# Weight-decoding arithmetic opened to GpSimd, with another hand-written order, in an attention and gated-MLP kernel

## The chip, the cores and the metric

The kernel runs on one core of one Trainium2 chip. The metric is device time in microseconds (us); lower is better. TensorE is called PE, VectorE DVE, ScalarE ACT, GpSimd POOL and the engine that issues most transfers SP. The kernel before was timed three times.

## The reference, cut to what matters

Attention over 8 batches, 8 heads, 576 positions and 64 channels per head, with a decay that is summed along the sequence, and then a gated MLP on the 512 joined channels:

```python
cum = np.cumsum(np.log(np.clip(f, 1e-4, 1.0)), axis=-1)
scores = q @ k.T / 8 + cum[:, None] - cum[None, :]      # causal, then a softmax
x = attn @ v                                            # (8, 576, 512) over all heads
gate = sigmoid(sum_k conv_w[k] * shifted(x, k))         # 5 taps along the sequence
out = (gate * (x @ w_val)) @ w_out
```

`w_val`, `w_out` (both 512 x 512) and `conv_w` (5 x 512) arrive as 64-bit floats, which no engine computes with. The kernel reads each as two 32-bit words and makes of them a high and a low 32-bit part, so that products can be taken in three passes of the fast `fp32r` format.

## The kernel before, in words

The 64 (batch, head) rows are 32 pairs of heads, i = 0 to 31; four pairs make one batch. For a pair, PE makes scores in PSUM banks (class S), DVE adds the decay and finds each row's minimum ("red", line 457), ACT takes exponentials (SX, line 461), PE transposes them (PT, lines 502 and 526), ACT or DVE copies the transposes out of PSUM (class PE, line 259), PE multiplies by v (PV), and DVE scales the result into `x` (line 576). From pair 4 on the loaded q and k (`Xr`) are first split into `Xh` (TH, a cast, line 259) and `Xl` (TL, a subtraction, line 373). `x` is split likewise into `xh` and `xl` (line 583). The convolution (cv, lines 264, 266 and 615) and a tanh give the gate. After four pairs the MLP of a batch follows: first product (Mv), gating (line 647), a split into `hh` and `hl` (line 661), second product (Mo), a copy out (O) and a store. "sel" (lines 466, 468 and 301) writes the causal mask into a loaded decay tile.

`decode` and `plan_w` unpack the weights, in eight chunks of 128 x 512 (four of `w_val`, class wv, then four of `w_out`, class wo). For one chunk: "low" (line 704, ACT) converts the low words, "m" (706, DVE) masks bits, "mid" (708, DVE) adds the two, "y" (710, DVE) masks the high words, "expo" (712, ACT) scales them, "h" (714, DVE) and line 716 (DVE) build the high part and its power of two, then "hi" (a cast, line 259, ACT or DVE) and "lo" (line 741, POOL or DVE) write the parts into `wall`. `conv_w` goes through the same `decode` with 20 columns (class cw). All chunks share the scratch tiles `wz` and `wh`, so they follow one another.

Nothing decides at run time: `plan.add` collects 2932 nodes with the engines that may run each (`dve`, `act` and `pool` allow one, `any_` several, with a duration in us), and `Plan.order` replays TABLE, a string that names for each of its 2572 entries the node, its engine and its PSUM bank. Each engine therefore works through a fixed queue, and waits at its head for whatever a node depends on. The durations in the code are not read when the table is replayed.

Of the kernel before, what the change touches and what calls it, by code (L numbers as in the profile page):

```python
# [9 lines left out]
I32 = mybir.dt.int32  # L10
AF = mybir.ActivationFunctionType
# [34 lines left out]
0010s30240z40930740K40r30V40d30C20B10D20E20t30520630430F10G20e20b30m000H20f10I20a30J20q010h20u30c328002340i20j40N20M12R40P22900O20Q10g10R22a02d22j0565  # L46
740T10S25942b22e10U32f22c12s012q22h20x32g11442o22t02k20X13-42m22p10Y22642i10-22x0700Z20_10p032u22n12l11022r12v11122A0342z21332D065121340122C22E12B12F2
1f42y12w21721612G043722V037602H13b23523c12I41921822K41a12X04642Q11b22W03811c21d12M43021e33613i022O43223112-24241h13k042Y24043311q43921k23a11i21l13x001
1j22Z13d051m22_13j23e03z15543l21n23o114443A0473f24844c33C11p33B13p22T43y13m14b037403q21B43g13n33r21s13u0561o13s25j33w14d24x013v14f24e13h24m0654g14h34a
34i20y34B0377044k24j14C24n34l14o23D034D14q23O003E14p14s23H43N14t21v23F44u14y24r15d45i043761t24z17244v21u23L41w17f24H0123J44w15k24I15b40l054J14A25l14E0  # L50
215m27441x24K044G14U14F25o33Q017g37d15r25n14L25p24O45t0425s11y20v34M43P25u35q15I0355h37645v21z13R25E065x25K13U205z34S45J17e30n053S15F27840o034Q43V25G1
8b47i35A23W27h053673T35B15f45w15C28h43t13X25y14V041A37l25D17j27m15H21D13Y27n35O0237c35Q10w37k15P25R004W25L0325S17q25_15T44X051E25N15V47o25M11F21M47r17
s0341G27p14Y27t37H0275X48q34_107w27u25Z47D057J15028j47I17y36k078d47v18r37z27E27A19m462025127F18f47B27x152260037C14Z17G25321H14-37K0456327N0066127L17Q0
17R16426c037P17U47O27-16526f068o17S48n27a41I266106d09q48p31K16g06727Y47M16e26n025419o46h29z16827W48s063546i19u41J28t23Z19s46j38u26o06928v16l01L38w29B1
7_066p28x18y36m29A38B281078z28C16a26q18E38028A19C38D0408228S05285168H2ax48F26s038U19E31X48628J38T18O019y38318726r38G16t08P21O16v058K28438Q1882az46w08L
16u26b18M21R29D01234aB48N16x2aK38I18l4892aM1aD48Y0059H28Z19Z068-19F29I19O0058R29G19-29J3aL3cB49M28V0219_19K28X18W28_069P39N16D01902aP39Q26y19349S26A02
9R19929149U39T1aF49X26B01P29Y19V29L11Q2cD4a10549W1aN2a70679741S16E0a02954a811T2a919w4a31aO006376z2a21cQ11U26F2aJ3aa041V1cO3aQ29c01ak1aS2ab2aT1aU36C2ae
49a04cR3aV2ac49d2aW1aX2cF46G1a40169b2a-3aR11W3aZ0329g24a51dM4b12a61bc001a_2cJ4aY19h2b33ai4be16H3b806b429i2ag4b511Z1cH4al01b629j2cP3b71dQ4bd1b92aH4b019
k2ba1bf003cT31-2b21cS04567202bh1bb2dZ2bg11_2211bi032an00cW2d-3bk1cU2cX1am2bj1cL4d1025cY3cV1ao2222dS4bl00dO4bm2bv16N03cN2cZ2eX4ar10c_2bn42326I04d01as2d
23bp4c-1253d52241d32dc06at2d41d736O0d_1d82da2d61au2e03d916J0dd2db1av2de1f34br49e2dg0528a1e22e101067bt46K19f3di2e_46P1f14dj024df26Q4e32fa3by03dk1dU4dl1  # L60
e526L4dh1e73bw02e61ea2e82eb1bz2ec005e91ed2bx2ap1dp03g64ee2dm076eg2ef16S02eZ4dz2ei3dn1e41fb26T0do1el2dY3dq2bC16ej2dr4bA1bD2dt4en03eh1f81bE26X01em1eo2f9
3ek1dv46Y0bF2ep1dx46U1bG2fd3ga4aq3er034g84fc02567et2es16Z1gl3eu040fe2dA03fg2ff1eq2fh1fi3dC01bB3dB2ev1fj2ew1fl2ex032dD2eA04fo2ey1fn010dE2eK1eB2gj1f72eC
4fr2bL03ez2fk1eE4fp2bI05fs1dW4ft3fm1gm3bM0i54dG16f54bJ0bN29l1eG4fw2gk3dH2bQ04bK2fy02dI2bO1bT05fu2fx1fz2bP3fv1bR0fq1dJ2id4fA1bU0eI4dF3dK2i94fC010bV2i74
gn06723bS2fD1go3ge4fB2bW2gc4fF015gr26V4eL04gp26-4gs1fG2gt3fE1eN07gu2gq1eM2gw2ii2gy064gx1eO2gz3fL00aw1fH2ik3jg4fI073gv1gC2bY05gg4gA2fV1bX2bZ0bH1gE2fM1b
_02fJ2ij3eR10fP4gF2b-2ib4c707gB1gH2eS2gG1fN4c00gI1in3gD1gi3eT2c406il3fK1c12gJ03eU2c21c50fT4dL1gK2jt3fR4c80eV2gL1ji4c32gN052jk4im03401gO1gM2c92c62jv2gQ
# [754 lines left out]
```

## Time and profile before

| | us |
|---|---|
| median of three runs | 496.66 (496.4 to 498.02) |
| the profiled execution | 495.69 |
| span of its instructions | 494.0 |
| PE busy | 473.0 |
| DVE busy | 430.0 |
| ACT busy | 345.6 |
| POOL busy | 192.1 |

The profiled execution is 1.69 us longer than its span, and 0.97 us shorter than the median. A row of a view by lines gives line, engine, operation, output<-inputs, shapes, count, then busy us and mean ns of one, then the engine's idle time just before and what ended it. PE's busy time counts modelled ends of pipelined matmuls, so a PE that is shown busy can still be held up between them.

### The profile page before, as it was taken

Reading aid. Unit: us, or ns where it says so; the run is one execution under the profiler, and the core shown is the slowest. Engines: PE = TensorE matmul, PEld = TensorE weight load, DVE = VectorE, ACT = ScalarE, POOL = GpSimd, SP = SyncE. Lnnn points to the kernel's source line nnn. Section 1 sums busy time; section 2 is a strip of 40 time slices with the busy share of each in tenths; the row PEclk is TensorE's granted clock in tenths of the full one; section 3 lists DMA queues with packets and bytes.
Section 4 is the critical chain, followed back from the end, with each engine's and each line's share of the span. In section 5 each row is a group of like instructions: output and inputs, shape, how many; then the busy total and the mean of one; then the engine's idle time right before and its main releaser. Section 6 shows DMA issues by size and latency. Waiting matters only on the chain.

```text
span 494.0 us, 13906 instructions
## 1 busy us (share of the span) xinstructions
PE 473.0 (96%) x5136; PEld 411.3 (83%) x5136; DVE 430.0 (87%) x1181; ACT 345.6 (70%) x937; POOL 192.1 (39%) x249
## 2 busy tenths in 40 slices
PE   5898999899999999999999999999999999999996
PEld 3666788778899888998898888998889988998985
DVE  5999999999889889989899999979998989988661
ACT  4999989898867767578687667577887776662010
POOL 4242748564554642272334423144312644340100
PEclk9999999999999999999999999999999999999999
DMA  5785665576365456555663474744636474510112
GB/s 183 248 262 160 196 200 197 149 210 201 135 205 203 124 150 227 133 175 175 161 176 94 146 225 159 226 131 152 202 90 195 156 195 137 191 53 27 42 44 106
DMA packets 35012, 79.57 MB, mean 161 GB/s; under 512 B 5056, under 2 KB 5312, under 8 KB 34944
## 3 DMA queue, kind: packets, MB, share of 16 engines
q1 hardware_dynamic: 34864, 78.54, 52.3%
q8 instruction: 40, 0.66, 0.6%
q14 instruction: 28, 0.23, 0.2%
q10 hardware_dynamic: 80, 0.15, 0.1%
HBM read 68.93 MB, written 9.73 MB: 159 GB/s over the span
## 4 chain that ended last, share of the span: by engine, by line
PE 67%; DVE 12%; ACT 10%; DMA 6%; issue 3%; SPq 1%; POOL 1%; DVEq 0%; ACTq 0%; POOLq 0%
PE banks L244 59%; PE banks L502 6%; DVE banks L457 5%; ACT P L461 4%; ACT pt L259 2%; DMA x<-rzd 2%; PE banks L526 2%; DMA out_dram<-ot 1%; SPq L270 1%; DVE banks L615 1%; DVE negm L457 1%; DVE pt L259 1%; DMA rzd<-pl 1%; DMA Xr<-in_x_dram 1%; ACT Pl L461 1%
## 5 line engine op out<-in xcount | busy, mean ns | idle before, releaser
L461 ACT ACTIVATE P<-banks,negm 128x512 f32<-128x512 f32 (+3 forms) x256 | 134.0, 529 | 37.6 <-DVE negm L457 36.6
L457 DVE CUSTOM_DVE_ANT_0 banks<-banks,dm 128x512 f32<-128x512 f32 (+1 forms) x240 | 115.3, 504 | 11.6 <-POOL dm L466 3.6
L244 PE MATMUL banks<-xh,wall 128*128 128x288 f32 x512 | 110.7, 299 | 0.5 <-DVE pt L259 0.5
L259 ACT COPY pt<-banks 128x512 f32<-128x512 f32 (+1 forms) x163 | 81.2, 532 | 27.7 <-PE banks L502 19.5
L466 POOL TENSOR_SCALAR_AFFINE_SELECT dm<-dm 128x256 f32<-128x256 f32 x83 | 35.8, 433 | 160.4 <-DVE negm L457 121.6
L244 PE MATMUL banks<-pt,vt 128*64 128x128 f32 (+1 forms) x1280 | 93.5, 297 | 1.7 <-DVE h L647 1.3
L244 PE MATMUL banks<-wall,hh 128*128 128x512 f32 x288 | 91.0, 397 | 0.5 <-DVE x L576 0.4
L244 PEld LDWEIGHTS banks<-xh,wall 128*128 128x128 f32 x512 | 84.2, 188 | 3.0 <-DVE pt L259 0.8
L244 PEld LDWEIGHTS banks<-pt,vt 128*64 128x64 f32 x1280 | 75.5, 137 | 10.4 <-ACT P L461 1.9
L615 DVE SCALAR_TENSOR_TENSOR banks<-x,cw,banks 128x576 f32<-128x576 f32 x96 | 78.5, 817 | 2.5 <-ACT banks L264 1.7
L373 POOL TENSOR_TENSOR Xl<-Xr,Xh 128x640 fp32r<-128x640 f32 (+1 forms) x44 | 66.5, 1516 | 34.3 <-ACT Xh L259 19.4
L244 PE MATMUL banks<-xl,wall 128*128 128x288 f32 x256 | 75.5, 295 | 0.0
L502 PEld LDWEIGHTS banks<-ident,P 64*128 64x128 f32 x1280 | 49.5, 138 | 18.3 <-ACT P L461 6.2
L502 PE MATMUL banks<-ident,P 64*128 64x64 f32 x1280 | 58.1, 226 | 6.0 <-ACT P L461 2.9
L244 PEld LDWEIGHTS banks<-wall,hh 128*128 128x128 f32 x288 | 51.9, 188 | 11.2 <-DVE x L576 0.5
L244 PE MATMUL banks<-wall,hl 128*128 128x512 f32 x144 | 56.3, 391 | 0.0
L461 ACT ACTIVATION_READ_ACCUMULATOR P<-banks,negm 128x1 f32 x256 | 51.9, 203 | 0.0
L244 PE MATMUL banks<-Xh 64*128 64x512 f32 (+2 forms) x224 | 51.8, 375 | 0.1
L244 PEld LDWEIGHTS banks<-xl,wall 128*128 128x128 f32 x256 | 48.1, 188 | 0.3
L244 PE MATMUL banks<-Xh,Xl 64*128 64x512 f32 (+2 forms) x224 | 45.9, 327 | 0.5 <-POOL Xl L373 0.3
L583 POOL TENSOR_TENSOR xl<-x,xh 128x576 fp32r<-128x576 f32 x24 | 34.3, 1431 | 29.6 <-DVE xh L259 22.2
L244 PE MATMUL banks<-Xl,Xh 64*128 64x512 f32 (+2 forms) x224 | 45.6, 325 | 0.0
(97 smaller groups left out, 758.3 us busy)
## 6 DMA issues: line engine op xcount, KB each, us to landing
Xr<-in_x_dram SPq DMA_DIRECT2D x32, 608.0 KB
dm<-decd SPq DMA_DIRECT2D x60, 256.0 KB
vt<-in_v_dram SPq DMA_DIRECT2D x32, 320.0 KB
x<-rzd SPq DMA_DIRECT2D x64, 144.0 KB
out_dram<-ot SPq DMA_DIRECT2D x36, 256.0 KB
dl<-decd SPq DMA_DIRECT2D x60, 144.0 KB
ot<-in_w_val_dram SPq DMA_DIRECT2D x2, 512.0 KB
wu<-in_w_val_dram SPq DMA_DIRECT2D x2, 512.0 KB
```

The source lines that it names most:

```text
L244: nc.tensor.matmul(out, lhsT=lhsT, rhs=rhs, start=start, stop=stop)
L259: (eng.copy if eng is nc.scalar else eng.tensor_copy)(out=out, in_=in_)
L270: lambda e: (nc.sync if e == "SP" else nc.scalar).dma_start(out=out, in_=in_), reads, writes, **kw)
L373: eng.tensor_tensor(out=Xl[r][:, a:e], in0=Xr[r][:, a:e], in1=Xh[r][:, a:e].bitcast(F32), op=ALU.subtract)
L457: nc.vector.tensor_tensor_reduce(out=sl, in0=sl, in1=add, op0=ALU.add, op1=ALU.min, scale=-0.125, scalar=3.0e38, accum_out=negm[r][:, col])
L461: nc.scalar.activation(out=dst[:, o:o + ext], in_=bank(key)[:, c0:c0 + ext], func=AF.Exp, bias=negm[r][:, col], scale=-1.0, accum_out=zs[r ...
L466: eng.affine_select(out=t, in_=t, pattern=[[0, 2], [-1, P]], base=0, channel_multiplier=1, compare_op=ALU.is_ge, fill=-BIG)
L502: nc.tensor.transpose(out=bank(key[a])[:, c:c + D], in_=Pt[ms[h]][sl, BOFF[b] + P * j:BOFF[b] + P * j + P], identity=ident[sl, sl])
L526: nc.tensor.transpose(out=t[0:m, 512 * h + D * j:512 * h + D * j + D], in_=Pl[r][sl, P * j:P * j + m], identity=ident[sl, sl])
L583: any_("xl", {"POOL": 1.4, "DVE": 0.67}, p, lambda eng: eng.tensor_tensor(out=xl[s], in0=xv, in1=xh[s][:, :].bitcast(F32), op=ALU.subtract ...
L615: eng.scalar_tensor_tensor(out=gt if n == KC - 1 else sums, in0=src, scalar=wt_, in1=sums, op0=ALU.mult, op1=ALU.add)
```

## The change

Three of `decode`'s steps may run on POOL too, and the casts "hi" and the entries for TH and "lo" get other durations in the planner's terms. The load of `conv_w` gets another due time. The table is another one: of the 2572 entries 286 name another engine, and order and banks differ.

```diff
-            any_("TH", {"ACT": c / 1200.0 + 0.09, "DVE": c / 1920.0 + 0.08, "POOL": c / 640.0 + 0.42}, i + 0.02 * n, hi, [("Xr", r)], [("Xh", r, n)])
+            any_("TH", {"ACT": c / 1200.0 + 0.09, "DVE": c / 1920.0 + 0.08, "POOL": c / 1280.0 + 0.27}, i + 0.02 * n, hi, [("Xr", r)], [("Xh", r, n)])
...
-        act(cls, a, p, lambda: nc.scalar.activation(
-            out=zz, in_=y.bitcast(mybir.dt.uint32), func=AF.Copy, scale=2.0 ** -52), kl + kg, kz)
+        g = n / 1280.0 + 0.25
+
+        def low(eng):
+            if eng is nc.scalar:
+                eng.activation(out=zz, in_=y.bitcast(mybir.dt.uint32), func=AF.Copy, scale=2.0 ** -52)
+            else:
+                eng.tensor_scalar(out=zz, in0=y.bitcast(mybir.dt.uint32), scalar1=2.0 ** -52, scalar2=None, op0=ALU.mult)
+
+        def mid(eng):
+            if eng is nc.vector:
+                eng.scalar_tensor_tensor(out=zz, in0=m, scalar=2.0 ** -20, in1=zz, op0=ALU.mult, op1=ALU.add)
+            else:
+                eng.tensor_scalar(out=h, in0=m, scalar1=2.0 ** -20, scalar2=None, op0=ALU.mult)
+                eng.tensor_tensor(out=zz, in0=h, in1=zz, op=ALU.add)
...
+        any_(cls, {"ACT": a, "POOL": g}, p, low, kl + kg, kz)
...
-        dve(cls, two, p, lambda: nc.vector.scalar_tensor_tensor(
-            out=zz, in0=m, scalar=2.0 ** -20, in1=zz, op0=ALU.mult, op1=ALU.add), kh + kz + kg, kz)
+        any_(cls, {"DVE": two, "POOL": g + n / 440.0 + 0.1}, p, mid, kz + kg, kz + kh)
...
-        act(cls, a, p, lambda: nc.scalar.activation(
-            out=y, in_=y, func=AF.Relu, scale=8.0, bias=ebias[0:y.shape[0]]), [*kl, ("ebias",)], kl)
+        any_(cls, {"ACT": a, "POOL": 2 * g}, p, expo, [*kl, ("ebias",)], kl)
...
-        load("cw", 0.1, p, cwu, conv_w.bitcast(I32), (), [("cwu",), ("h32", 1), *kl])
+        load("cw", 0.31, p, cwu, conv_w.bitcast(I32), (), [("cwu",), ("h32", 1), *kl])
...
-            any_(nm, {"ACT": 0.52, "DVE": 0.34}, p, lambda eng, hi=hi: copy(eng, hi, wh), kh + kg, [(nm + "h", c)])
+            any_(nm, {"ACT": 0.55, "DVE": 0.34, "POOL": 0.67}, p, lambda eng, hi=hi: copy(eng, hi, wh), kh + kg, [(nm + "h", c)])
```

Read entry by entry, the two tables differ in engines as follows (out and back in, whole table; in brackets the part ahead of the first Mo, entry 637 of before and 636 of after):

| class | ACT to POOL | DVE to POOL | POOL to ACT | POOL to DVE | ACT to DVE | DVE to ACT |
|---|---|---|---|---|---|---|
| low, 128 x 512 | 5 (5) | | | | | |
| low, 20 columns | 1 (1) | | | | | |
| hi, 128 x 512 | 2 (2) | | | | | |
| mid, 128 x 512 | | 1 (1) | | | | |
| TH | 15 (3) | 6 (1) | 6 (1) | | 3 | 5 (1) |
| TL | | 12 (1) | | 10 (1) | | |
| hl and xl | | 13 | | 9 | | |
| sel | | 31 (4) | | 29 (5) | | |
| class PE, 512 columns | | | | | 23 (1) | 27 (3) |
| class PE, 256 columns | | | | | 9 | 13 (2) |
| class PE, 73 x 128 | | | | | 7 (1) | 11 (3) |
| cv | | | | | 5 | 6 (1) |
| O, hh, xh | | | | | 18 | 18 |

The step "expo" stays on ACT everywhere. One 64-column copy of the mask at the start goes from POOL to DVE. On SP the load of `conv_w` becomes the first one, ahead of the half of `f` that was first. On POOL the 20-column "low" stands ahead of the making of `ident`. In PE's queue the number of neighbours that use the array in different ways (the planner's `mode`) is 238 before and 233 after.

## Rows read from the trace of the kernel before

**Rows 1.** The page's head and its first part, whole span.

```profile
span 494.0 us, 13906 instructions
PE 473.0 (96%) x5136; PEld 411.3 (83%) x5136; DVE 430.0 (87%) x1181; ACT 345.6 (70%) x937; POOL 192.1 (39%) x249
```

**Rows 2.** Windows: stretch, its length, busy us (count) of PE, PEld, DVE, ACT, POOL.

```profile
10.00:110.00 100.00, 91.49 (x1072) 73.73 (x1071) 94.39 (x275) 91.18 (x244) 49.32 (x60) 1.00 0.67 201
110.00:440.00 330.00, 326.45 (x3674) 289.94 (x3673) 298.63 (x824) 242.35 (x668) 133.09 (x161) 1.00 0.55 166
440.00:494.00 54.00, 50.24 (x380) 44.58 (x378) 32.03 (x73) 8.95 (x22) 4.29 (x4) 1.00 0.14 51
```

**Rows 3.** The chain that ended last, by line: from 10 to 110, then 120 to 450.

```profile
by line: PE banks L244 25.8%; DVE banks L457 11.7%; ACT P L461 10.8%; DMA x<-rzd 7.9%; ACT pt L259 5.9%; issue 5.7%; PE banks L502 3.8%; ACT Pl L461 3.2%; DVE banks L615 2.7%; DVE negm L457 2.2%; DVE gate L615 1.9%; DMA rzd<-pl 1.6%; ACT ba
...
by line: PE banks L244 66.0%; PE banks L502 7.4%; DVE banks L457 3.4%; issue 3.1%; ACT P L461 2.7%; PE banks L526 1.9%; ACT pt L259 1.8%; DMA out_dram<-ot 1.8%; DMA Xr<-in_x_dram 1.1%; SPq L270 1.0%; DMA dm<-decd 1.0%; DMA dl<-decd 0.8%; DV
```

**Rows 4.** The start: pieces of that chain, SP's first issue, PE's second stretch.

```profile
1.44 3.07 DMA h<-in_conv_w_dram
4.54 0.89 DVE gate L706
9.17 0.52 DVE gate L335
...
0.81 0.58 SPq L270 DMA_DIRECT2D Pl<-in_f_dram  x1
...
10.33 2.29 PE L244 MATMUL banks<-gate,gate 64*128 64x512 f32 x12
```

**Rows 5.** ACT's groups by line and form, whole span.

```profile
L704 ACT ACTIVATE gate<-ot 128x512 f32<-128x512 uint32 x4 | 2.8, 690 | 0.8 <-DMA ot<-in_w_val_dram 0.8
L259 ACT CAST wall<-gate 128x512 fp32r<-128x512 f32 x8 | 5.0, 630 | 0.0
L259 ACT CAST Xh<-Xr 128x576 fp32r<-128x576 f32 x14 | 9.5, 676 | 0.0
L259 ACT COPY pt<-banks 128x512 f32<-128x512 f32 x118 | 66.9, 592 | 20.7 <-PE banks L502 12.7 <-DVE pl L259 3.2 <-PE banks L526 3.1
L259 ACT COPY pt<-banks 128x256 f32<-128x256 f32 x45 | 15.8, 374 | 7.0 <-PE banks L502 6.8
L264 ACT ACTIVATE banks<-x,cw 128x576 f32<-128x576 f32 x21 | 15.7, 749 | 1.2 <-DVE x L576 0.7 <-ACT P L461 0.2
```

**Rows 6.** DVE's groups by line and form, whole span.

```profile
L708 DVE SCALAR_TENSOR_TENSOR gate<-gate 128x512 f32<-128x512 int32 x8 | 5.5, 685 | 0.0
L259 DVE COPY pt<-banks 128x512 f32<-128x512 f32 x42 | 28.2, 683 | 2.9 <-PE banks L502 2.0 <-ACT pt L259 0.7
L259 DVE COPY pt<-banks 128x256 f32<-128x256 f32 x19 | 7.9, 416 | 0.0
L615 DVE SCALAR_TENSOR_TENSOR banks<-x,cw,banks 128x576 f32<-128x576 f32 x96 | 78.5, 817 | 2.5 <-ACT banks L264 1.7
L468 DVE TENSOR_TENSOR dm<-dm,tri 128x256 f32<-128x256 f32 x37 | 15.8, 427 | 0.5
```

**Rows 7.** POOL's groups by line and form, whole span.

```profile
L259 POOL CAST Xh<-Xr 128x576 fp32r<-128x576 f32 x9 | 6.1, 683 | 0.0
L741 POOL TENSOR_TENSOR wall<-gate,ot 128x512 fp32r<-128x512 f32 x4 | 5.2, 1297 | 10.7 <-DVE ot L716 10.7
```

**Rows 8.** Timeline near 5 us: a POOL fill, then a 20-column DVE step.

```profile
5.08 0.31 POOL L317 MEMSET gate<- 128x256 f32 x1
...
5.76 0.16 DVE L710 TENSOR_SCALAR h<-h 128x20 int32<-128x20 int32 x1
```

**Rows 9.** PE's timeline: the first product after transposes, and its successor.

```profile
87.82 0.40 PE L244 MATMUL banks<-xh,wall 128*128 128x288 f32 x1
88.06 0.30 PE L244 MATMUL banks<-xl,wall 128*128 128x288 f32 x1
```

**Rows 10.** PE's groups by line and form: the score products that read `Xl`.

```profile
L244 PE MATMUL banks<-Xh,Xl 64*128 64x512 f32 x56 | 11.5, 398 | 0.5 <-POOL Xl L373 0.3 <-DVE Xl L373 0.2
```

More of the change, by code (lines that the diff above doesn't have):

```diff
@@ L50 @@
[L50 to L53, printed above, removed]
@@ L98 @@
[L98 to L101 removed]
+0010b30z40240c30d30740r30K40V40630932R40C20B30430D20E20F10u30m000a30G20e20520f10q010H20x30I20g10J20h228002340t20i20M10N20j40P22902640O20Q12a00R22j0562
@@ L102 @@
+2DQ0Gy2HC01DM2Iq2Gz2HA02Gu2GA1HD2IA04DJ2Iu016IB1IK2Ir003IC4Iv1Fi2Ix045IE4Dq1Fj3Iz2DS01Fp1HB2Ea05DN1HE2It1II4DO2Iy1IG4DT0Iw1Is2HF3I-04HG22DR2E000DU2HH2
+IN07IL06IO2DV2HI2IX07IM2IP2DX01DW2IQ3J306E10I_0E21DY0E34J02HJ2E500DZ2HK2D-4Eb0IR12HL1IY0Je01IZ2IS2J607IT2Jb04J12J40J22J70Jc0J82J52E60J92IU2Jf0Ja2E71Ec
+1Jj07E84IV2Ed4Jm06Jd2IW1Jg2Jn0Jh2Ji2Jk0Jr01Jo2Jl2Jp2JG04Jq2Js0Jw06Jt2Ju4JB01Jx0JC0Jy2Jz4JL06JD1JE4JH0JM0JI2JJ4JN1JO4
 """
@@ L703, in decode, with expo @@
         a = n / 1200.0 + 0.145
-        act(cls, a, p, lambda: nc.scalar.activation(
-            out=zz, in_=y.bitcast(mybir.dt.uint32), func=AF.Copy, scale=2.0 ** -52), kl + kg, kz)
+        g = n / 1280.0 + 0.25
[10 more added lines that the diff above has]
+                eng.tensor_tensor(out=zz, in0=h, in1=zz, op=ALU.add)
+        def expo(eng):
+            if eng is nc.scalar:
+                eng.activation(out=y, in_=y, func=AF.Relu, scale=8.0, bias=ebias[0:y.shape[0]])
+            else:
+                eng.tensor_scalar(out=y, in0=y, scalar1=896.0 * 2.0 ** 20, scalar2=896.0 * 2.0 ** 20, op0=ALU.max, op1=ALU.subtract)
+                eng.tensor_scalar(out=y, in0=y, scalar1=8.0, scalar2=None, op0=ALU.mult)
+        any_(cls, {"ACT": a, "POOL": g}, p, low, kl + kg, kz)
         dve(cls, one, p, lambda: nc.vector.tensor_scalar(
             out=m, in0=hw, scalar1=0x1FF, scalar2=None, op0=ALU.bitwise_and), uk + kg, kh)
-        dve(cls, two, p, lambda: nc.vector.scalar_tensor_tensor(
-            out=zz, in0=m, scalar=2.0 ** -20, in1=zz, op0=ALU.mult, op1=ALU.add), kh + kz + kg, kz)
+        any_(cls, {"DVE": two, "POOL": g + n / 440.0 + 0.1}, p, mid, kz + kg, kz + kh)
         dve(cls, one, p, lambda: nc.vector.tensor_scalar(
             out=y, in0=hw, scalar1=0x7FFFFE00, scalar2=None, op0=ALU.bitwise_and), uk, kl)
-        act(cls, a, p, lambda: nc.scalar.activation(
-            out=y, in_=y, func=AF.Relu, scale=8.0, bias=ebias[0:y.shape[0]]), [*kl, ("ebias",)], kl)
+        any_(cls, {"ACT": a, "POOL": 2 * g}, p, expo, [*kl, ("ebias",)], kl)
         dve(cls, two, p, lambda: nc.vector.scalar_tensor_tensor(
@@ L739, in plan_w @@
             y = decode(nm, p, wu[w], wm, wz, wh, uk, kl)
-            any_(nm, {"ACT": 0.52, "DVE": 0.34}, p, lambda eng, hi=hi: copy(eng, hi, wh), kh + kg, [(nm + "h", c)])
-            any_(nm, {"POOL": 1.2, "DVE": DM / 960.0 + 0.075}, p, lambda eng, lo=lo, y=y: eng.tensor_tensor(
+            any_(nm, {"ACT": 0.55, "DVE": 0.34, "POOL": 0.67}, p, lambda eng, hi=hi: copy(eng, hi, wh), kh + kg, [(nm + "h", c)])
+            any_(nm, {"POOL": 1.25, "DVE": DM / 960.0 + 0.075}, p, lambda eng, lo=lo, y=y: eng.tensor_tensor(
                 out=lo, in0=wz, in1=y, op=ALU.mult), kz + kl + uk + kg, [(nm, c)])
```

104 lines of the change are left out of this document (52 added, 52 removed).

## The prediction

> **What bounds the kernel now.** The page comes first: PE is busy for 473.0 of 494.0 us, so at most 21 us could go without making PE's own work shorter [rows 1]. The windows then say where those 21 us lie. From 10 to 110 us, which holds the start of the pipeline and nearly all the decoding, PE is idle for 8.5 us while DVE is busy for 94.4 and ACT for 91.2 of 100: there all three are nearly full, and POOL, with 49.3, is not. From 110 to 440 PE idles 3.55 us of 330, with DVE at 90% and ACT at 73%. After 440 PE runs almost without a break to a last copy and store [rows 2]. What is left lies ahead of 10 us.
>
> The chain that ended last agrees. Between 10 and 110 us its rows of ACT's exponentials and copies make 19.9% (10.8 + 5.9 + 3.2), those of DVE 18.5% (11.7 + 2.7 + 2.2 + 1.9), those of PE 29.6%. Between 120 and 450 PE's two largest rows alone make 73.4%, DVE's row 3.4% and ACT's two 4.5% [rows 3]. So a microsecond taken from ACT or DVE counts in the first stretch and hardly afterwards. The first Mo, entry 637 of the table, comes at about the end of this stretch, so I divide the changed entries there.
>
> **The first stretch.** ACT gives up five "low" (5 x 0.690 = 3.45), two "hi" (2 x 0.630 = 1.26) and, net, one cast of `Xh` (0.68). It gets, net, two copies of 512 columns (1.18), two of 256 (0.75) and one convolution step (0.75) [rows 5]. That is 2.7 us less; steps under 0.3 us each, of both signs, are left out. DVE gives up one "mid" (0.69), two copies of 512 (1.37), two of 256 (0.83) and one convolution step (0.82), and gets two mask additions more (0.85) [rows 6]: 2.9 us less, and a little more with two casts of `Xh` that also leave it. The same engines are the two that are full.
>
> How much of it reaches the end? If only what lies on the chain counts, it is 19.9% of 2.7 and 18.5% of 2.9, together 1.1 us. If the stretch is as long as its fullest engine needs, it is the whole 2.9. Below that, a new order that makes other waits can take it all back; that is a rival. I take **2.0**, the middle, since DVE at 94% is nearer to full than to a chain's share [rows 2, 3].
>
> **What POOL pays.** No row shows "low" on POOL. Its floor is the one-input cast of 576 columns there (0.683, so about 0.61 for 512 columns); its ceiling is the two-input step on 512 columns (1.30) [rows 7]. It is nearest to the cast, having one input and 512 elements, though these lie 8 bytes apart; I take 0.65. The cover: by the new table "mid" or its DVE successor is at least ten entries behind its "low" for the full chunks, and an entry is 109/637 = 0.17 us here, so 1.7 us at the tightest place. The ceiling still fits. Without that cover DVE's queue would stand still for the excess, with the score minima behind "mid" and ACT's exponentials behind those. I add **0.2** for this, between 0 and 5 x 0.65 = 3.2. The single "mid" on POOL is two instructions, some 1.9 us by the same rows, and is covered likewise: 0. The two "hi" end in `wall`, which a product reads much later: 0, unless POOL's queue is late.
>
> **The start.** SP now issues `conv_w` first, one issue earlier: 1.44 - 0.81 = 0.63 us [rows 4]. Its landing leads the chain at the start (through DVE at 4.54 us to the decay at 9.17). PE reaches the decay products only at 10.33, behind the scores of pair 0, which another transfer sets, so PE's first stretch hides the gain [rows 4]; `f`, moved one issue back, is taken up after `conv_w` anyway. Behind it DVE and ACT still get to the minima and exponentials sooner. From 0 to 0.63 I take **0.3**. "low" for 20 columns now stands ahead of `ident` on POOL, where only PE's warm-up waits for it: 0.
>
> **PE's own order.** Where PE changes its kind of product, the next start comes after 0.24 us, against about 0.14 within a run [rows 9]. Five changes fewer are **0.5** us; bounds 0 and 0.5.
>
> **After 110 us.** DVE gets much lighter still: net two TL, four hl or xl, eight TH and twelve copies leave it over the whole table. But PE's idle time there is 3.55 us in all [rows 2], which bounds the gain from above; a new order can also lose. I take **0.5**. At the end the queues of PE have the same work in almost the same order: 0.
>
> **Collisions.** POOL gets some 27 us of work, 8 of it in the first stretch (priced by casts of 0.65 to 0.8, subtractions of 1.3 to 1.5). In the rows a 20-column step on DVE lasts 0.89 us while POOL fills tiles until 5.39, and ends at 5.43; the next step of that size lasts 0.16 [rows 4, 8]. So the two can hold each other up. The many "mid" and mask steps over the whole run, however, average what their columns need [rows 6]. I charge **0.5**, between 0 and 2.9. The Trainium skill, SBUF — State Buffer, section "Who interferes with whom", says that a DVE step in a two-port mode, which one-input casts and scalar steps can enter, and a POOL step exclude each other for a whole instruction. The early row agrees; if every new POOL step met such a DVE step, the sum would have 2.9 in place of this 0.5, as in the first rival.
>
> **The sum.** 2.0 + 0.3 + 0.5 + 0.5 - 0.2 - 0.5 = 2.6 us. Against the profiled 495.69 us this gives 493.1; the median is 0.97 higher, so the forecast is **494.1 us**. A measurement of this kernel can tell about 0.3% from no change, 1.5 us; "faster" is below 495.2, "slower" above 498.15.
>
> **Rival 1: the collisions take it back.** The first stretch gets net eleven POOL instructions. If each holds DVE for about 0.26 us, ACT's and DVE's relief of 2.9 us is gone, and 0.3 + 0.5 + 0.5 - 0.2 less what later collisions cost leaves 496 to 497 us: no change. For it: the 0.89 us row. Against: that row is one event, and such excess does not show in the means. Chance 0.17.
>
> **Rival 2: the gain is hidden.** 7.9% of the chain in the first stretch is the reciprocal's way through DRAM (`x`<-`rzd`) [rows 3], and PE's own rows are more; these don't shorten. Then only the 0.5 of PE's order is left, 496.2 us: no change. Chance 0.07.
>
> **Rival 3: POOL becomes a link, slower.** The place is `Xh`, then `Xl`, then the scores of a pair. POOL now makes 30 of the 56 casts (15 before), and each is followed by a subtraction of some 1.4 us behind it in the same queue. In the new table six pairs (8, 9, 12, 14, 23, 28) have their scores 5 to 11 entries behind a last subtraction on POOL; before it was two (13 and 15, at 11). At 494/2572 = 0.19 us an entry that is 1.0 to 2.1 us, about the length of that subtraction. If POOL runs late, four of them by 1.5 us each cost 6 us, and 494.1 + 6 is **500 us**. It decides from the point where POOL lags by over 0.6 us at more than two of these places (3.0 us gives back the gain). For it: PE has waited for POOL's `Xl` before, 0.3 us [rows 10]. Against: that is all in 56 such products, and POOL will still be idle over half the time. Chance 0.15.
>
> **Rival 4: a first use halts POOL.** "low" is the first plain scalar step there, and the 20-column one lies on the start's chain, where each us of a halt at about 4.5 us adds one. It decides from 4.1 us, the forecast's gain of 2.6 and the 1.5 that can be told: 498.2 us. Against: the rows show no such halt; the four subtractions of line 741, the first POOL arithmetic of the decoding among them, have no idle time before them but waits for DVE [rows 7]. Chance 0.03. The Trainium skill, GPSIMD Engine Reference, section 2.1 "Instruction dispatch", says that the first call to a freshly loaded routine costs about 6 us that no instruction shows; by that the time would be 500.
>
> **How the numbers follow.** The forecast has 0.58, rivals 1 and 2 together 0.24 (no change), rivals 3 and 4 0.18 (slower). The forecast's own range: at best 2.9 + 0.63 + 0.5 + 1.5 of the later 3.55 = 5.5 us, 491 us; at worst the chain's share of 1.1 and the larger charges, about 495.5. The range for 8 in 10 goes from 490.5 up through both no-change rivals and into rival 3, where half of its price stands: 498.5.
>
> **What would show it.** In the changed profile, from 10 to 110 us: ACT near 89 and DVE near 91 for the same work, or the same shares with the first Mo at about 107 instead of 109.2 us. "low" on POOL near 0.65 us. The early 20-column steps about 0.6 us sooner. Collisions would show as longer means of DVE's casts and scalar steps; rival 3 as waits of PE for POOL's `Xl` of over a microsecond in sum; rival 4 as a POOL step or gap of several microseconds before `ident`. The forecast is wrong if the first Mo comes no sooner, or comes sooner and PE's idle time after 110 us grows past 3.55 us by as much.

## The result, and the profile after

The changed kernel takes **500.6 us** (median, 497.14 to 502.94) beside 497.15 for the kernel before on the same chip (495.77 to 498.6): the ratio is 1.0066, 95% interval 1.0039 to 1.0093. It is slower by 0.7%; the forecast was 494.1, faster, with a range up to 498.5. Of the twelve executions the four with a mean granted clock of PE of 0.995 or more took 497.1 to 500.2 us, and the eight at 0.992 or 0.993, the profiled one with 502.1 among them, 499.6 to 502.9. So the traces show more than the loss: their spans differ by 6.4 us, while the ratio of the times gives 3.3.

The page's head and first part, of the changed kernel:

```profile
span 500.4 us, 13931 instructions
PE 474.9 (95%) x5136; PEld 414.0 (83%) x5136; DVE 426.7 (85%) x1153; ACT 343.4 (69%) x934; POOL 223.3 (45%) x281
```

Against [rows 1] DVE has 3.3 us less to do, ACT 2.2 less and POOL 31.2 more, where I had counted 27. The work did leave the two full engines, and the span still grew. The windows, with the columns of [rows 2] (the third number from the end is PE's granted clock):

```profile
10.00:110.00 100.00, 89.91 (x1032) 72.68 (x1028) 92.18 (x257) 85.24 (x233) 57.93 (x69) 0.97 0.63 192
110.00:440.00 330.00, 323.62 (x3635) 288.20 (x3636) 292.90 (x798) 237.40 (x658) 152.92 (x184) 1.00 0.56 164
```

PE's idle time in the long stretch went from 3.55 to 6.38 us, and in the first stretch from 8.51 to 10.09. The first Mo (PE's timeline) begins 3.6 us later than the 109.16 of before:

```profile
112.74 0.73 PE L244 MATMUL banks<-wall,hh 128*128 128x512 f32 x2
```

Put side by side at equal progress of PE's work (the products of each table summed at full clock), the changed kernel is some 2 us ahead at about 18 us, level with the old one at about 38, 3.8 behind at 54 and still 3.6 at the first Mo. It wins back 2 us between 240 and 275, and loses 5.1 between 306 and 462. So there are two places to explain, 40 to 54 us and the second half.

POOL's groups by line and form show the first surprise. (Lines have moved: "low" is 708 on ACT and 710 on POOL, "mid" 714 on DVE and 716 with 717 on POOL, "m" 726, "y" 729, "lo" 759.)

```profile
L710 POOL TENSOR_SCALAR gate<-wu 128x512 f32<-128x512 uint32 x3 | 4.8, 1593 | 0.3
L710 POOL TENSOR_SCALAR gate<-ot 128x512 f32<-128x512 uint32 x2 | 3.1, 1529 | 0.2
L716 POOL TENSOR_SCALAR gate<-gate 128x512 f32<-128x512 int32 x1 | 1.5, 1490 | 0.8 <-DVE gate L726 0.8
L259 POOL CAST wall<-gate 128x512 fp32r<-128x512 f32 x2 | 1.2, 612 | 0.0
L710 POOL TENSOR_SCALAR gate<-h 128x20 f32<-128x20 uint32 x1 | 0.3, 261 | 0.1
```

"low" takes 1.53 to 1.59 us, not 0.65, and more than the ceiling of 1.30. Its reading every second word is not the reason: line 716, also a multiplication from 32-bit integers, reads its input without gaps and takes 1.49. The 20-column one, the first of all, lasts 0.26 us, and POOL stands idle for less than 0.1 us before it.

The second surprise stands in DVE's groups:

```profile
L468 DVE TENSOR_TENSOR dm<-dm,tri 128x256 f32<-128x256 f32 x28 | 15.7, 562 | 0.2
L476 DVE TENSOR_SCALAR Pl<-zs 128x9 f32<-128x9 f32 x32 | 8.9, 277 | 1.2 <-ACT P L461 0.9 <-ACT Pl L461 0.2
L714 DVE SCALAR_TENSOR_TENSOR gate<-gate 128x512 f32<-128x512 int32 x7 | 6.1, 868 | 0.0
L615 DVE SCALAR_TENSOR_TENSOR banks<-x,cw,banks 128x576 f32<-128x576 f32 x96 | 78.6, 819 | 3.8 <-ACT banks L264 3.0
L259 DVE COPY pt<-banks 128x512 f32<-128x512 f32 x38 | 25.7, 681 | 1.1 <-PE banks L502 0.4 <-ACT pl L259 0.3 <-PE banks L526 0.3
```

The mean of the mask step (468) has gone from 427 to 562 ns and that of "mid" from 685 to 868 [rows 6]; the 817 of the convolution step and the 683 of the copy out of PSUM are where they were. The steps that grew have all their operands in SBUF; those that did not read or write a PSUM bank (`banks`). The timeline shows how a mean grows, here with POOL's, DVE's and PE's lines of one place (start, length, engine, line, and in brackets an idle time and what ended it):

```profile
41.95 3.32 POOL L373 TENSOR_TENSOR Xl<-Xr,Xh 128x576 fp32r<-128x576 f32 x2
...
42.23 1.64 DVE L729 TENSOR_SCALAR ot<-ot 128x512 int32<-128x512 int32 x1
43.78 2.03 DVE L714 SCALAR_TENSOR_TENSOR gate<-gate 128x512 f32<-128x512 int32 x1
45.74 0.68 DVE L457 CUSTOM_DVE_ANT_0 banks<-banks,dm 128x512 f32<-128x512 f32 x1
...
47.35 0.53 PE L526 MATMUL banks<-ident,Pl 64*128 64x64 f32 x9 [1.61 <-ACT P L461]
47.83 2.83 PE L244 MATMUL banks<-pt,vt 128*64 128x192 f32 x16
```

While POOL's two subtractions run, from 41.95 to 45.27, DVE does one scalar step and one "mid", which end 0.3 and 0.5 us behind one subtraction each: 3.6 us for what elsewhere takes 1.1. The score minima (line 457) behind them start at 45.74, ACT's exponentials wait for these, and PE waits 1.61 us for ACT. To measure this over the run I sum, for all DVE instructions, what each lasted beyond the median of its own form, where that is over 0.15 us. This **held sum** is 6.0 us in the kernel before (0.7 of it in the first 110 us) and 14.3 in the changed one (4.9 in the first 110). Of the twelve holds of over 0.5 us after, ten fall on a subtraction `Xl` on POOL, one on a cast of `Xh` and one on "mid" there. Eleven casts, scalar steps and two-input steps of DVE on SBUF tiles began while an `Xl` subtraction ran on POOL, and ten of them were held; of the 85 steps with a PSUM operand that did so, none was.

The third: after its wait PE runs at half its clock. Windows of the changed kernel:

```profile
18.00:20.00 2.00, 0.84 (x19) 0.65 (x18) 1.89 (x5) 2.00 (x5) 0.76 (x1) 1.00 0.48 183
20.00:22.00 2.00, 1.98 (x13) 0.98 (x9) 2.00 (x11) 2.00 (x7) 0.54 (x1) 0.61 0.01 2
22.00:24.00 2.00, 2.00 (x10) 1.49 (x8) 1.70 (x7) 1.67 (x7) 0.00 (x0) 0.54 0.53 166
...
48.00:50.00 2.00, 2.00 (x14) 1.51 (x16) 1.97 (x7) 2.00 (x6) 0.00 (x0) 0.50 0.03 8
```

Behind PE's gaps at 18 and 45.5 us (1.16 and 1.61 us) the granted clock of these windows is 0.50 to 0.61, that is the lower of its two levels, 1.2 GHz, for most of the time, and "busy" PE there does half the work. The old kernel has a gap of 1.24 us at 17.5 us and stays at 1.00.

### The profile page after: what moved, and what is told of

It is laid out like the page before. It is cut to its first block, busy times and chain, and to the rows that moved or that the text cites. A ratio compares the mean times of both kernels' runs of the same rounds, so it can differ in the third digit from the quotient of the medians.

```text
span 500.4 us, 13931 instructions
## 1 busy us (share of the span) xinstructions
PE 474.9 (95%) x5136; PEld 414.0 (83%) x5136; DVE 426.7 (85%) x1153; ACT 343.4 (69%) x934; POOL 223.3 (45%) x281
## 4 chain that ended last, share of the span: by engine, by line
PE 60%; DVE 7%; issue 4%; ACT 4%; DMA 3%; POOL 3%; SPq 0%; DVEq 0%; POOLq 0%; ACTq 0%
PE banks L244 54%; PE banks L502 5%; ACT P L461 2%; DVE banks L457 2%; DMA vt<-in_v_dram 1%; PE banks L526 1%; DVE banks L615 1%; ACT pt L259 1%; DMA Xr<-in_x_dram 1%; DMA dm<-decd 1%; DVE pt L259 1%; DVE dm L468 1%; POOL dm L466 1%; POOL hl L661 1%; DVE h L647 1%
## 5 line engine op out<-in xcount | busy, mean ns | idle before, releaser
L259 ACT COPY pt<-banks 128x512 f32<-128x512 f32 (+1 forms) x171 | 85.3, 528 | 37.8 <-PE banks L502 30.5
L466 POOL TENSOR_SCALAR_AFFINE_SELECT dm<-dm 128x256 f32<-128x256 f32 x92 | 40.0, 436 | 140.3 <-DVE negm L457 113.3
L244 PE MATMUL banks<-pt,vt 128*64 128x128 f32 (+1 forms) x1280 | 94.8, 299 | 2.7 <-DMA vt<-in_v_dram 1.3
L373 POOL TENSOR_TENSOR Xl<-Xr,Xh 128x576 fp32r<-128x576 f32 (+1 forms) x46 | 69.0, 1509 | 2.8 <-ACT Xh L259 2.5
L502 PE MATMUL banks<-ident,P 64*128 64x64 f32 x1280 | 56.9, 226 | 3.7 <-ACT P L461 2.0
L583 POOL TENSOR_TENSOR xl<-x,xh 128x576 fp32r<-128x576 f32 x23 | 34.1, 1485 | 31.2 <-DVE xh L259 29.0
```

Of the source, the lines that this page charges most:

```text
L244: nc.tensor.matmul(out, lhsT=lhsT, rhs=rhs, start=start, stop=stop)
L259: (eng.copy if eng is nc.scalar else eng.tensor_copy)(out=out, in_=in_)
L373: eng.tensor_tensor(out=Xl[r][:, a:e], in0=Xr[r][:, a:e], in1=Xh[r][:, a:e].bitcast(F32), op=ALU.subtract)
L466: eng.affine_select(out=t, in_=t, pattern=[[0, 2], [-1, P]], base=0, channel_multiplier=1, compare_op=ALU.is_ge, fill=-BIG)
L502: nc.tensor.transpose(out=bank(key[a])[:, c:c + D], in_=Pt[ms[h]][sl, BOFF[b] + P * j:BOFF[b] + P * j + P], identity=ident[sl, sl])
L583: any_("xl", {"POOL": 1.4, "DVE": 0.67}, p, lambda eng: eng.tensor_tensor(out=xl[s], in0=xv, in1=xh[s][:, :].bitcast(F32), op=ALU.subtract ...
```

## Experiments

Three theories, not exclusive. **L**: "low" at 1.55 us on POOL delays the decoding, and what follows it. **C**: POOL's reading of SBUF holds DVE's SBUF steps, and the new order makes more of these meetings in places that count. **K**: the new order's gaps on PE lower its clock. The kernels are named after the order (table) that they start from; each ratio is to the kernel before on the same chip. In edits of a table the lines stand for its entries.

### Parts of the change

**Nine decoding steps back** on ACT and DVE, in the new order (after_decode_back), and **the same nine alone on POOL**, in the old order (before_decode_pool):

```diff
-low (six), hi (two), mid (one): POOL
+low (six), hi (two): ACT, mid (one): DVE
```

> The changed table, with its nine decoding steps on GpSimd (six low, two hi, one mid) put back on ScalarE and VectorE in the same places of the order; the 21 casts of Xh and the rest stay on GpSimd. Theory L (low lasts 1.55 us on GpSimd, where the prediction had 0.65, and sets back what follows it in that queue): the loss goes, about 497 us, and PE has no gap of over 1 us between 42 and 48 us. Theory C (GpSimd's subtractions and casts of SBUF tiles hold VectorE's steps that read SBUF): most of the loss stays, 499 to 501. Theory K (gaps of PE early on bring TensorE's clock down): the granted clock tells; 1.000 here if the gaps came from low, and then 497 to 498.

> The old table with nothing but the nine decoding steps moved to GpSimd, in the same places of the old order. Theory L: 1.5 to 4 us slower than before (498.5 to 501), since the old order puts mid one to twelve entries behind low for the first chunks; PE's early gaps grow. Theory C: five steps of 1.55 us more on GpSimd hold VectorE a few times, 0.5 to 1.5 us slower. Theory K: slower only if the granted clock falls below 1.000.

Measured: 502.65 us, ratio 1.0131 (1.0105 to 1.0156), held sum 12.4; and 498.89 us, 1.0061 (1.0037 to 1.0084), held sum 6.9. So the nine steps cost 0.6% in the old order, and taking them out of the new one doesn't bring it back: the new order is slow without them too.

**The casts of `Xh` as before** (after_th_back), everything else as changed:

```diff
-TH: the engines of the new table
+TH: the engines of the old table
```

> The changed table with every cast of Xh (TH) put back on the engine that it had before; decoding stays on GpSimd. Theory C: VectorE is held less, the sum of what its steps last over their usual time falls from 14 us toward the 6 us of before, and the time falls by 2 to 4 us to 497 to 499. Theory L: no gain, 500 to 501. Theory K: about 500 with a granted clock of 0.993 if the two stretches at half clock stay.

Measured: 501.32 us, 1.0087 (1.0061 to 1.0113), held sum 10.9. The fifteen added casts are not the loss. Without them it is 0.4 us ahead of the kernel before at 116 us, 1.3 ahead at 275, and loses 5.4 from there to 477.

### What one POOL step costs DVE

**81 subtractions that nobody waits for** (before_idle_sub): the old kernel, and in 29 places where POOL stands idle, up to four subtractions of 384 columns into a scratch tile; and its control, **two memsets for each** (before_idle_memset):

```diff
+        for _ in range(spots.get(k, 0)):
+            nc.gpsimd.tensor_tensor(out=scr.rearrange("p (a b) -> p a b", b=P), in0=tri4[:, None, :].to_broadcast([P, 3, P]),
+                                    in1=ident[:, None, :].to_broadcast([P, 3, P]), op=ALU.subtract)
...
+        for _ in range(2 * spots.get(k, 0)):
+            nc.gpsimd.memset(scr, 0.0)
```

> The old kernel with 81 subtractions of 384 columns more on GpSimd, into a scratch tile that nobody reads, put where its queue stood idle for 1.9 us or more; no engine waits for them. Theory C (GpSimd's reads of SBUF hold VectorE's steps that read SBUF): VectorE's held time, 6 us in the old trace, at least doubles, and the kernel gets slower by 2 to 5 us though nothing depends on the new work. If it stays within 1 us, GpSimd's load as such is harmless, and the loss of the changed kernel comes from its order or from late results.

> The control of the dose: the old kernel, with two memsets of 384 columns for each of the 81 idle subtractions of the earlier run, in the same idle places of GpSimd (some 162 x 0.42 = 68 us of GpSimd in place of 87). They write SBUF and read nothing. Theory C, in the form that GpSimd's two-input reading holds VectorE: within 0.5% of the kernel before, 496 to 498 us, and VectorE's held sum stays near 6 us. Rival: any access of GpSimd to SBUF, or its queue being full, costs the same: 505 to 510 us.

Measured: 510.26 us, **1.0283** (1.0263 to 1.0303), held sum 27.0; the memsets 497.76 us, 1.0022 (1.0007 to 1.0036), held sum 9.0. The groups of the run with subtractions:

```profile
L769 POOL TENSOR_TENSOR scr<-tri,ident 128x384 f32<-128x384 f32 x81 | 87.4, 1080 | 4.1
...
L615 DVE SCALAR_TENSOR_TENSOR banks<-x,cw,banks 128x576 f32<-128x576 f32 x96 | 78.4, 817 | 2.3 <-ACT banks L264 1.5
L468 DVE TENSOR_TENSOR dm<-dm,tri 128x256 f32<-128x256 f32 x37 | 23.4, 633 | 0.5
```

and of the run with memsets:

```profile
L769 POOL MEMSET scr<- 128x384 f32 x162 | 69.7, 430 | 7.7
...
L468 DVE TENSOR_TENSOR dm<-dm,tri 128x256 f32<-128x256 f32 x37 | 15.8, 428 | 0.5
```

C is shown as a mechanism: work that is on no chain, in idle time of POOL, costs 14 us, 0.18 us a step, when it reads SBUF, and 1.1 us in all (0.3 to 1.8) when it writes only. Late results of POOL don't explain the 14 us: the largest wait for POOL that grew, that of the score minima for the mask step on POOL (line 466), is 4.9 us beside 3.6 before. The mask step on DVE, two SBUF inputs, goes from 427 to 633 ns beside reads and stays at 428 beside writes; the convolution step with its PSUM operand keeps 817. The Trainium skill, SBUF — State Buffer, section "Who interferes with whom", says just this of the two inputs: such a DVE step contends with a GpSimd instruction that reads SBUF, not with one that only writes it. These runs agree. Writing does hold something, though: of 18 casts and scalar steps that began on DVE beside one of these memsets 7 ended over 0.15 us late, of 26 two-input steps none, and the held sum is 9.0 in place of 6.0. For one-input steps the two runs don't compare reading with writing, since a memset lasts 0.43 us and a subtraction 1.08.

### Is it the length of "low"?

**"low" as a plain conversion on POOL** (before_decode_pool_cast, old order with the nine steps there; after_low_cast, the changed kernel):

```diff
-                eng.tensor_scalar(out=zz, in0=y.bitcast(mybir.dt.uint32), scalar1=2.0 ** -52, scalar2=None, op0=ALU.mult)
+                eng.tensor_copy(out=zz, in_=y.bitcast(mybir.dt.uint32))
```

> As the old table with nine decoding steps on GpSimd, but low there is a plain conversion without the factor 2^-52, so the low parts of five weight chunks and of conv_w come out without that factor. Theory L (the 1.55 us of low are the loss of that kernel): if the conversion lasts about 0.65 us like the other casts, the time comes back by 1.5 to 2.5 us to 496 to 497.5. Theory C: a shorter step holds VectorE less as well, but the loss sits in other steps; 498 to 499. If the conversion of 32-bit integers itself is slow, it lasts about 1.5 us too and nothing changes.

> The changed order, with the step low on GpSimd as a plain conversion to float32, without its factor 2^-52 (so the output is not the reference's). In the old order the conversion took 0.66 us where the scaling step takes 1.5. Theory L (the long step delays the decoding, and with it everything after): 6 x 0.85 us less on GpSimd before 110 us; most of the 3.5 us lost there returns, 497 to 498 us (ratio 1.000 to 1.003). Theory C (what costs is GpSimd's reading of SBUF in all the run): the late loss of some 3 us stays, and the early one too, since it sits on the subtractions, not on low: 499 to 500.5 us (1.004 to 1.007).

POOL's group of the first:

```profile
L710 POOL CAST gate<-wu 128x512 f32<-128x512 uint32 x3 | 2.0, 657 | 0.2
```

Without the factor the step takes 0.66 us from the same strided words: what I had forecast holds for a conversion, not for a multiplication. The output lacks the factor in both kernels. The times: 496.91 us, 1.0011 (0.9999 to 1.0023), where it was 1.0061; and 497.93 us, **1.003** (1.0014 to 1.0046), where it was 1.0066. So L is real: 0.5% in the old order, and some half of the loss in the new one (where the two intervals just overlap). But the held sum stays at 12.3, and the kernel is still slower than before.

### Is it the holds?

**Ten subtractions off POOL** (after_unheld): the `Xl` that were running in the holds at 42 to 45, 91, 328 to 330, 378, 392, 410 and 428 to 431 us. And **both edits** (after_unheld_cast):

```diff
-TL, ten entries: POOL
+TL, ten entries: DVE
```

> The changed order, with ten subtractions Xl (at 42 to 45, 91, 328 to 330, 378, 392, 410 and 428 to 431 us) on VectorE instead of GpSimd: those that were running while VectorE's steps were held, 10.9 us of VectorE's time together. They cost VectorE 10 x 0.86 us in place of the holds. Theory C: VectorE's time is nearly the same, but its steps on the path no longer stop for 1.2 us at a time, and GpSimd has 15 us more room: 497 to 498.5 us (ratio 1.000 to 1.004), the gain behind 300 us and at 45 us. Theory L: the decoding is no sooner: 500 us (1.006). If holds simply come up at other places: 500 us with a held sum of over 12 us.

> Both edits at once: ten subtractions off GpSimd, and low as a plain conversion (output not the reference's). If L and C each hold a part of the loss, the two add up: 493.5 to 496 us (ratio 0.995 to 1.000), and the gain at the start that was forecast is seen at the end. If one of them is empty, this is no faster than the better of the two single edits.

Measured: 494.56 us, **0.9967** (0.9949 to 0.9984), held sum 2.5; and 493.5 us, **0.9939** (0.9923 to 0.9954), held sum 3.3. The first leaves nothing out (the second leaves out the factor of "low"), and beats both the old and the changed kernel. The place shown above, now in after_unheld:

```profile
42.66 0.41 DVE L729 TENSOR_SCALAR ot<-ot 128x512 int32<-128x512 int32 x1
42.99 0.68 DVE L714 SCALAR_TENSOR_TENSOR gate<-gate 128x512 f32<-128x512 int32 x1
43.59 0.69 DVE L457 CUSTOM_DVE_ANT_0 banks<-banks,dm 128x512 f32<-128x512 f32 x1
...
44.87 0.88 PE L526 MATMUL banks<-ident,Pl 64*128 64x64 f32 x10
45.71 1.52 PE L244 MATMUL banks<-pt,vt 128*64 128x192 f32 x16
```

The two steps end at 43.67 in place of 45.81, PE has no wait ahead of line 526, and its 16 products take 1.52 us in place of 2.83, since the clock stays at 1.00 there. The page and the windows:

```profile
PE 471.9 (96%) x5136; PEld 412.8 (84%) x5136; DVE 421.5 (86%) x1163; ACT 343.1 (70%) x934; POOL 209.1 (42%) x271
...
10.00:110.00 100.00, 91.83 (x1072) 74.87 (x1071) 93.92 (x270) 88.69 (x244) 56.25 (x68) 0.98 0.63 196
110.00:440.00 330.00, 326.12 (x3684) 291.88 (x3683) 292.98 (x819) 238.73 (x663) 142.24 (x176) 1.00 0.55 165
```

DVE took over ten steps and is busy 5.2 us less, for what it lost in the holds was more. At equal progress the two runs are within 0.7 us of each other up to 45 us; after_unheld is 3.2 ahead at 54 us, 3.7 at 275 and 7.5 at 462: the two places to be explained.

**Does the old order gain as much?** (before_unheld): its five two-input subtractions that DVE waited for, on DVE. And the nine decoding steps on POOL in that (before_unheld_decode_pool):

```diff
-xl (one), TL (three), hl (one): POOL
+xl (one), TL (three), hl (one): DVE
```

> The old order, with its five two-input subtractions that VectorE waited for (one xl, three Xl, one hl) on VectorE. Theory C: the held sum falls from 6 to about 3 us, and the time by 0.5 to 2 us: 494.5 to 496.3 us (ratio 0.996 to 0.999). If only the changed order gains by such an edit, since its holds lie on the path and the old order's do not: 496 to 498 us (0.999 to 1.003).

> The same old order without its five, and the nine decoding steps on GpSimd. In the old order with its holds they cost 2.3 us (ratio 1.0061). Theory L (the length of low delays the decoding): the same 2 to 3 us over the old order without the five, so 497 to 499 us. Theory C (the loss is in the meeting of low and the subtractions with VectorE): less than 1 us over it, 495 to 496.5 us.

Measured: 496.28 us, 1.000 (0.9986 to 1.0013), held sum 3.8; and 499.65 us, 1.0071 (1.0048 to 1.0094), held sum 4.7. The old order gains nothing: its holds were off the path, or worth no more than the five steps that DVE took over. And the steps on POOL cost it as much without these holds as with them, so that in the old order their loss is L's, as the conversion showed.

**The decoding's part in the order without holds** (after_unheld_decode_back): after_unheld, with the nine steps back on ACT and DVE.

```diff
-low (six), hi (two), mid (one): POOL
+low (six), hi (two): ACT, mid (one): DVE
```

> The changed order with the ten subtractions on VectorE, and the nine decoding steps back on ScalarE and VectorE. If the move of the decoding is worth what was forecast (2.0 us in the first stretch), this is slower than the same order with the steps on GpSimd: 496 to 497 us (ratio 0.9995 to 1.0015). If the step low on GpSimd, at 1.5 us, gives nothing, 494 to 495 us (0.995 to 0.9985). If the move is a loss by itself, under 493.5 us.

Measured: 495.59 us, 0.9973 (0.9954 to 0.9993), held sum 2.7. The move is worth 0.0006 as it was made, which can't be told from nothing. With "low" at the price of a conversion it is 0.9973 - 0.9939, 1.7 us, with intervals that just touch.

### Is it PE's clock?

**More or moved idle transposes**: 38 added ahead of the transposes that follow the gaps (after_warm); three of the existing groups of such transposes moved there (after_warm_moved); and the old kernel without four of its groups (before_no_warm):

```diff
+                if (i, n_) in ((2, 1),):
+                    for k in range(6):
+                        nc.tensor.transpose(out=bank(key[0])[:, k % 4 * P:k % 4 * P + P], in_=ident, identity=ident)
...
+            if i in (0, 2):
+                for k in range(16):
+                    nc.tensor.transpose(out=t[:, k % 8 * P:k % 8 * P + P], in_=ident, identity=ident)
...
-        for n in range(NB):
+        for n in range(NB if wk[1] in (1, 5) else 0):
```

> The changed kernel with 38 more transposes of the identity on PE, into banks that the next instruction of PE's queue overwrites, where PE stood waiting: 16 ahead of the last transposes of pair 0, 6 and 16 ahead of two groups of pair 2. Nothing else changes. Theory K: the granted clock is 1.000 and the time falls by 2 to 3.5 us, to 497 to 498.5. Theories C and L: PE's products no longer run at half clock there, but what held the other engines is untouched; less than 1 us, 499.5 to 500.5.

> The changed table with three of its own groups of four warm-up transposes moved: one from 31 us to PE's gap at 18 us, two from 53 us to its gap at 45.5 us. No instruction more or less. Theory K (the clock falls after gaps of PE and costs time): mean granted clock 0.996 to 1.000 in place of 0.993, and 497.5 to 499 us. Theory C alone: 500 to 501 whatever the clock.

> The old kernel without the four groups of warm-up transposes that it has between 16 and 51 us. Theory K: the granted clock falls below 0.997 in nearly every run, and 2 to 4 us are lost, 498.5 to 500.5, though PE has 1.8 us less to do. If a lower clock costs nothing here because other engines set the pace: 495.5 to 497.

Measured: 502.95 us, 1.0127 (1.0098 to 1.0156); 498.98 us, 1.0053 (1.0035 to 1.007); 496.72 us, 1.0016 (1.0001 to 1.003). The first added 5.1 us of PE work, and says nothing of K. In the second the clock is 1.00 in both places; its ratio lies under the changed kernel's, but within its interval, so the times don't decide. Its trace does part the clock from the hold at 45 us, in one execution: "mid" is still held, the clock behind it is 1.00, and the first Mo comes 1.4 us earlier than the changed kernel's 112.74, where without the holds (after_unheld, 109.06) it comes 3.7 earlier:

```profile
43.30 1.90 DVE L714 SCALAR_TENSOR_TENSOR gate<-gate 128x512 f32<-128x512 int32 x1
...
48.00:50.00 2.00, 2.00 (x38) 1.81 (x34) 1.97 (x7) 1.96 (x7) 0.00 (x0) 1.00 0.00 1
...
111.39 0.73 PE L244 MATMUL banks<-wall,hh 128*128 128x512 f32 x2
```

For the gap at 18 us, once more without the holds: **one group moved into the gap at 18 us** (after_unheld_warm), where after_unheld still ran at 0.62 and 0.53.

```diff
-warm, fourth group: at its old place in PE's queue
+warm, fourth group: ahead of the last transposes of pair 0
```

> The changed order without its holds (after_unheld, 494.56 us, 0.9967), and one of the existing groups of idle transposes moved ahead of the transposes at 19.2 us, where TensorE stands idle for 1.2 us and then runs at 0.53 to 0.62 of its clock until 24 us. Theory K: the gap is filled, the clock stays at 1.00 and the first long score products take 1.75 us in place of 3.4; 1.5 to 2 us come back, 492.5 to 493.5 us (ratio 0.992 to 0.9945). Rival: ScalarE and VectorE set the pace of that stretch, TensorE waits for them anyway, and the time stays at 494 to 495 us.

Measured: 495.24 us, 0.9974 (0.9953 to 0.9996). PE's timeline of it:

```profile
19.37 0.66 PE L341 MATMUL banks<-ident 128*128 128x128 f32 x4 [1.17 <-ACT Pl L461]
...
20.57 1.83 PE L244 MATMUL banks<-Xr 64*128 64x512 f32 x6
```

where after_unheld has (and its window, then the same window with the group moved)

```profile
20.25 3.39 PE L244 MATMUL banks<-Xr 64*128 64x512 f32 x7
...
20.00:22.00 2.00, 1.98 (x13) 0.98 (x11) 2.00 (x9) 2.00 (x6) 0.56 (x1) 0.62 0.01 2
...
20.00:22.00 2.00, 2.00 (x25) 1.40 (x26) 1.88 (x8) 1.73 (x5) 0.69 (x1) 1.00 0.00 0
```

The clock stays at 1.00 in all windows from 18 to 26 us and six of the score products take 1.83 us, where seven took 3.39, and yet both kernels are level by 30 us and the time is the same. ACT and DVE are each busy for 3.7 of the 4 us from 18 to 22, and set the pace there. K costs nothing that can be told at this place. At 48 us the half clock can have cost 1.7 us of PE's work at most (0.06, 0.50 and 0.29 of three windows of 2 us), and 1.4 of the 3.7 us by the execution above; the rest goes with the holds.

## Why the prediction was wrong

**The collisions were mis-sized, and this turned the sign.** I charged 0.5 us, between 0 and 2.9. Removing the ten meetings is worth 1.0066 - 0.9967, some 4.9 us, after DVE pays for ten subtractions and with the half clock at 48 us that went with them. Two arguments failed. "The means average what their columns need" was true of [rows 6] and told of the old order's few meetings, not of the price of one: a DVE step that meets a POOL subtraction waits for its end, up to 1.4 us, and not the 0.26 of rival 1. And the upper bound took only the new POOL steps of the first stretch, while 9.5 of the 14.3 us held lie after 110 us, and most of the holds are on subtractions that were on POOL before as well: nine of the ten moved in after_unheld. What had changed for them was what stood beside them on DVE. The prediction's "after 110 us", a gain of 0.5, was a loss for that reason.

**"low" was mis-sized**: 1.55 us in place of 0.65, above the ceiling of 1.30, since neither row that I took as a bound is an integer input with a multiplication. The cover was miscounted too. "mid" stands ten entries behind at the tightest place, but "y", which overwrites the words that "low" reads, stands seven and nine entries behind it in two chunks, 1.2 and 1.5 us, and there DVE waits for POOL, 0.50 and 0.26 us:

```profile
27.58 0.43 DVE L729 TENSOR_SCALAR wu<-wu 128x512 int32<-128x512 int32 x1 [0.50 <-POOL gate L710]
```

With the conversion these waits are gone, and the charge of 0.2 is some 1.4 us (0.9967 - 0.9939, intervals that overlap a little).

**The first stretch's 2.0 us** didn't come, even without holds and with a short "low". The forecast's own sign, a first Mo at about 107 us, is in no run of the new order. It starts here in after_unheld, in after_unheld_cast and in after_unheld_decode_back, beside 109.16 before:

```profile
109.06 0.73 PE L244 MATMUL banks<-wall,hh 128*128 128x512 f32 x2
...
109.12 0.73 PE L244 MATMUL banks<-wall,hh 128*128 128x512 f32 x2
...
110.21 0.73 PE L244 MATMUL banks<-wall,hh 128*128 128x512 f32 x2
```

So the move of the nine steps is worth about 1.1 us at that place, and the rest of the new order gives as much back there. In the times it is worth 0.3 us as the change made it, which can't be told from nothing, and 1.7 with "low" at 0.66 us. That after_unheld_cast, at 0.9939 or 493.6 us on the 496.66 of the forecast, ends so near to the 494.1 is luck: at equal progress it is 0.3 us ahead of the kernel before at 150 us, 3.2 at 275 and 1.4 at 462, so its gain arises after 110 us, where I had put 0.5.

**The start** came more than forecast and didn't last. `conv_w` is there at 2.56 us in place of 4.54 [rows 4], and DVE then waits for the 20-column "low", which POOL takes up only behind other steps of its queue, at 4.29. I had put that at 0:

```profile
4.58 0.18 DVE L714 SCALAR_TENSOR_TENSOR gate<-gate 128x20 f32<-128x20 int32 x1 [1.85 <-POOL gate L710]
```

The 20-column "y" is at 4.68 in place of 5.76 us and the decay's step at 8.20 in place of 9.17 [rows 4, 8], while PE's first decay products are at 10.33 as before; at 18 us the kernel leads by some 2, at 38 by nothing. The row that I took for a collision there, 0.89 us beside a fill, looks like one: it ends 0.03 us behind the fill. In before_no_warm that step lasts 0.18 us, and it is the 20-column "y", begun during the fills, that ends 0.04 us behind them, and in the run with 162 memsets both get by with 0.18 and 0.28:

```profile
4.74 0.69 DVE L710 TENSOR_SCALAR h<-h 128x20 int32<-128x20 int32 x1
...
5.08 0.31 POOL L317 MEMSET gate<- 128x256 f32 x1
```

**The rivals.** Rival 1 named the mechanism and, with the Trainium skill's rule, its reach ("exclude each other for a whole instruction"), but I priced it by the means and gave it 0.17; and the rule as I told it left out the two-input steps, which are six of the twelve long holds. Rival 3 did not happen: PE's products that read `Xl` never wait, where before they had 0.5 us [rows 10]:

```profile
L244 PE MATMUL banks<-Xh,Xl 64*128 64x512 f32 x56 | 11.4, 391 | 0.0
```

The end of 500 us that it gave is right, and its reason wrong. What did grow is another wait for POOL, that of the score minima for the mask step, here before and after (us in all, times, longest):

```profile
DVE banks L457 <- POOL dm L466: 3.6, 9, 0.8
...
DVE banks L457 <- POOL dm L466: 8.6, 19, 1.2
```

In after_unheld, which is faster than the old kernel, it is still 7.4 us in 18 places, so it isn't what the ten subtractions cost; what it costs by itself was not tried. Rival 4 did not happen either: 0.26 us for the first "low", and no gap before it. Nor did rival 2, for there was a loss, not a hidden gain. PE's 0.5 us for changes of mode was not tried.

**Open**: how much of the loss at 45 to 54 us is the half clock's in the times (the traces give at most 1.7 us); whether the lower clock makes the longer executions of the changed kernel long; and why after_decode_back, with nearly the same holds, is slower than the changed kernel by 0.65% when the same edit costs 0.06% without holds (its profiled execution took 498.43 us beside the median of 502.65, so its trace doesn't show it).

## What to carry to other kernels

A step moved to an idle POOL is not free when it reads SBUF: look which DVE steps stand beside it, and count casts, scalar steps and two-input steps without a PSUM operand as stopped until POOL's instruction ends (ten of eleven were here). A mean of the old order doesn't show that price; one meeting in the timeline does. And price a step by a row with its own operation and types: a conversion's row doesn't bound a multiplication.

## What the hardware showed that I had not expected

- A scalar step from 32-bit integers on POOL takes 1.49 to 1.59 us for 512 columns, strided or not; a conversion of the same words 0.66, a cast of floats 0.61.
- How long DVE is held doesn't set the time by itself: held sums of 6.0 and 3.8 us give the same time in the old order, while 14.3 against 2.5 is worth 1% in the new one, where at 45 us the score minima stand behind the held steps.
- PE's granted clock fell behind a gap of 1.16 us (0.61 and 0.54 in two windows of 2 us), with no effect on the time that can be told where ACT and DVE were the pace.
- Fills on POOL, which only write, held some casts and scalar steps of DVE (7 of 18) and no two-input step (0 of 26).
